# Batch 0 of an attention and expert kernel: summed values brought to their rows by products on TensorE in place of a trip through memory

## The chip, the cores and the metric

The kernel runs on one core of a Trainium2 chip. The metric is device time in microseconds of one execution; the number that counts is the median of several.

## What is computed

The reference first does attention with keys and values that are pooled over eight neighbouring positions, then a two-level mixture of experts on the result. Cut to what matters here:

```python
def _attn_ref(q, k, v):                       # 8 batches, 8 heads, 576 positions, 64 wide
    k_p = k.reshape(B, H, Sp, pool, D).mean(axis=3)      # Sp = 72
    v_p = v.reshape(B, H, Sp, pool, D).mean(axis=3)
    scores = scale * np.matmul(q, k_p.transpose(0, 1, 3, 2))
    ...softmax over the 72 pooled keys...
    return np.matmul(attn, v_p)

def _moe_ref(x, w_group, w_expert, w1, w2):   # x: 4608 tokens, 512 wide
    g_idx = np.argmax(x @ w_group, axis=1)
    ...
        e_idx = np.argmax(xg @ w_expert[g], axis=1)
        ...
            h = np.maximum(xg[mask_e] @ w1[g, e], 0.0)
            out[tok_idx] = combined[:, None] * (h @ w2[g, e])
```

## The kernel before

The eight batches are worked one after the other, and their stages overlap: while batch b runs its expert (class Moe), batch b+1 runs its attention (class Att). For each batch one expert is picked as the main one, and all of the batch's tokens go through it; the few tokens that belong elsewhere are handled at the end by class Left. The expert's two layers are computed at more than single fp32r precision: each weight and each activation is split into a rounded high part and a low part (tiles `wh`, `wl`, and the two halves of `xa` and `xb`), and three products, high by high, low by high and high by low, are summed.

The order of work on every engine is written out by hand, in the strings START, FIRST, SECOND, STEADY and LAST. Each word is a step: `a.sc:0` is method `sc` of batch 0's attention on query chunk 0, `m.` is the expert of the same batch, `n.` the next batch. Each engine works through its own instructions strictly in that order.

The change touches START, which has no expert of an earlier batch to run beside batch 0's attention. The steps of batch 0 there, with the lines of the kernel before, are:

- `vr` (L276, L277, L289, VectorE): sums the values in groups of eight. For batch 0 the sums land in `vf` (a part of a tile named ht), 128 flat rows to a chunk, five chunks; the last chunk begins at row 448.
- `guess_x`, `guess_e` (L508, L516 on TensorE, L511 on ScalarE, L519 to L502 on VectorE): guess the main expert from `vf`. The result `me` is read by SyncE, and only then are the expert's weights loaded (`m.load`, L573, tile sw).
- `home_v` (L224 to L229): brings the sums from `vf` into `v6` (named v in the trace), where each quarter of the 128 partitions holds the rows of two heads, in five groups of 32. The kernel before writes `vf` to memory (vscr) by three SyncE transfers and reads it back by four that ScalarE issues. ScalarE's four wait for the write, so whatever stands behind them on ScalarE waits too.
- `qt` (L315, L311 on TensorE, L317 on ScalarE): turns the queries. `sc` (L336): scores. `mx`, `sb` (L348, L357 on VectorE, L362 on ScalarE): maximum, difference and exponential of a chunk; `sb` is `sd` (the difference) followed by `ex` (the exponential).
- `su_` (L368 to L370, VectorE), `nm` (L375, GpSimd), `pt` (L382, VectorE): sum, norming, transposition of a chunk into pT.
- `vm` (L294, GpSimd): two small products on `v6` that `av` reads.
- `warm:4` (L947): four products of ones with ones, whose result nobody reads.
- `av:0` (L396, TensorE; L401, ScalarE; `avd`, L412, VectorE): the attention's result for the first 256 tokens, tile xa, high and low part.
- `cast` (L579, ScalarE) and `lo` (L585, GpSimd): split a quarter of a weight into its high and low part.
- `m.up` (L602): first layer of the expert; the step of feature block f needs weight quarter f // 2.

GpSimd's order around the change is: `nm` of chunks 0 and 1, `vm`, `lo` of weight quarters 0 and 1, `nm` of chunk 2, `lo` of quarter 2, `nm` of chunk 3, `lo` of quarter 3, `nm` of chunk 4, then the sums of batch 1's values (L276, L277, L289) and batch 1's `vm`, which batch 1's `guess_x` on TensorE reads.

Of the kernel before, what the change touches and what calls it, by code (L numbers as in the profile page):

```python
# [8 lines left out]
F32 = mybir.dt.float32  # L9
# [8 lines left out]
B, H, S, D = 8, 8, 576, 64  # L18
SP = 72
# [15 lines left out]
LATE = 1  # L35
START = """
t.load_wr a.load_k:p a.load_q:0 a.load_vf a.load_q:1 a.load_q:4
t.warm:10 t.turn_wr a.kr:0 a.kr:1 t.split_wr a.kt a.vr:0:f a.vr:1:f a.qt:0 a.qt:1 a.sc:0 a.mx:0 a.sc:1:m t.warm:2 a.guess_x a.sb:0 a.mx:1 a.home_v a.guess_e a.sb:1 a.qt:2 a.su_:0 a.nm:0:p
m.load:1:0 m.load:1:1 m.load:1:2 m.load:1:3 a.qt:3 a.su_:1 a.nm:1:p a.vm a.sc:2:m a.qt:4 t.warm:4 n.load_v n.load_k a.pt:0 a.pt:1 m.cast:1:0 m.lo:1:0:p:4 m.cast:1:1 m.lo:1:1:p:4
a.av:0 a.mx:2 a.sb:2 a.avd:0  # L40
"""
FIRST = """
m.up:0:0:1 a.su_:2 a.nm:2:p m.upd:0:0 a.sc:3 m.cast:1:2 m.load:2:0 m.up:1:0 a.mx:3 a.sb:3 m.lo:1:2:p:4 m.upd:1:0 a.pt:2 m.up:2:0 a.su_:3 a.nm:3:p m.cast:1:3 m.lo:1:3:p:4
m.load:2:1 m.load:2:2 m.upd:2:0 a.sc:4 m.up:3:0 a.mx:4 m.up:4:0 a.sb:4 m.upd:3:0 n.load_qb:0 n.load_qb:1 a.pt:3 a.su_:4 m.upd:4:0 a.nm:4:p m.load:2:3 n.load_qb:2 n.load_qb:3
m.up:5:0 a.pt:4 n.vr:0 m.upd:5:0 m.up:6:0 m.upd:6:0 m.up:7:0 a.av:1 n.vr:1 n.vm a.rt:0 m.upd:7:0 a.avd:1 n.kr:0
m.up:0:1:1 m.upd:0:1 n.kr:1 a.rt:1 n.guess_x m.cast:2:0 m.up:1:1 n.guess_e m.upd:1:1 a.route_g m.cast:2:1 m.up:2:1 m.upd:2:1 a.route_e:p a.gates m.lo:2:0:p:2 m.up:3:1 m.upd:3:1 m.lo:2:1:p:2 m.cast:2:2 m.up:4:1 n.qb:0 m.upd:4:1
# [33 lines left out]
def attn_moe(ctx: ExitStack, tc: tile.TileContext, q, k, v, wg, we, w1, w2, out):  # L80
    nc = tc.nc
# [3 lines left out]
    keep = ctx.enter_context(tc.tile_pool(name="keep", bufs=1))  # L85
    dram = ctx.enter_context(tc.tile_pool(name="dram", bufs=1, space=bass.MemoryType.DRAM))


    ident = keep.tile([128, 128], F32, name="ident")
    make_identity(nc, ident)  # L90
    ones = keep.tile([128, 128], F32, name="ones")
    nc.vector.memset(ones, 1.0)
    rowi = keep.tile([128, 2], F32, name="rowi")
# [48 lines left out]
    gate = keep.tile([128, B, NC], F32, name="gate")  # L142
    loh = keep.tile([128, B, NC, NE], F32R, name="loh")
    xscr = dram.tile([B, 128, 2, 4, S], F32, name="xscr")
    vscr = dram.tile([H * SP + 16, D], F32, name="vscr")

    w1v = w1.rearrange("g e (k p) f -> (g e) p k f", p=128)
    w2v = w2.rearrange("g e (k p) f -> (g e) p k f", p=128)
# [12 lines left out]
    ps_t = ctx.enter_context(tc.tile_pool(name="ps_t", bufs=3, space=PSUM))  # L161


    flat = lambda x: x.rearrange("p h d -> p (h d)")
# [15 lines left out]
    class Att:  # L180
# [40 lines left out]

        def home_v(s):

            nc.sync.dma_start(out=vscr[0:512].rearrange("(t p) d -> p t d", p=128), in_=s.vf[:, 0:4])  # L224
            nc.sync.dma_start(out=vscr[512:576], in_=s.vf[64:128, 4])
            nc.sync.dma_start(out=vscr[576:592], in_=s.vf[0:16, 0])
            for a in range(4):
                o = 2 * SP * a
                nc.scalar.dma_start(out=s.vtile()[32 * a:32 * a + 32, 0:5], in_=vscr[o:o + 160].rearrange("(j i) d -> i j d", i=32))  # L229

        def load_v(s, two=0):

# [768 lines left out]
```

## Time and profile before

| | us |
|---|---|
| median of 3 runs (514.2 to 516.41) | 515.48 |
| the profiled execution | 514.15 |
| its span, first to last instruction | 512.4 |
| TensorE busy in the span | 501.1 |
| GpSimd busy | 281.6 |
| VectorE busy | 345.6 |
| ScalarE busy | 206.3 |

Engines are named PE (TensorE), PEld (its weight loads), DVE (VectorE), ACT (ScalarE), POOL (GpSimd) and SP (SyncE) in the profile; a q behind the name is the engine's queue, which issues transfers. TensorE is busy almost throughout, so a change can save time where TensorE stands idle or repeats itself slowly, which is at the two ends of the span. [...]

### The profile page before, as it was taken

Reading aid. Unit: us, or ns where it says so; the run is one execution under the profiler, and the core shown is the slowest. Engines: PE = TensorE matmul, PEld = TensorE weight load, DVE = VectorE, ACT = ScalarE, POOL = GpSimd, SP = SyncE. Lnnn points to the kernel's source line nnn. Section 1 sums busy time; section 2 is a strip of 40 time slices with the busy share of each in tenths; the row PEclk is TensorE's granted clock in tenths of the full one; section 3 lists DMA queues with packets and bytes.
Section 4 is the critical chain, followed back from the end, with each engine's and each line's share of the span. In section 5 each row is a group of like instructions: output and inputs, shape, how many; then the busy total and the mean of one; then the engine's idle time right before and its main releaser. Section 6 shows DMA issues by size and latency. Waiting matters only on the chain.

```text
span 512.4 us, 14902 instructions
## 1 busy us (share of the span) xinstructions
PE 501.1 (98%) x6085; PEld 440.1 (86%) x6085; DVE 345.6 (67%) x928; ACT 206.3 (40%) x385; POOL 281.6 (55%) x246
## 2 busy tenths in 40 slices
PE   8899999999999999999999999999999999998996
PEld 6688987998889978899789988899789988898976
DVE  6876877899385869486784768476784764199702
ACT  2354432545216542455216551455325551344212
POOL 2386666576518595476828585476947471830400
PEclk9799999999999999999999999999999999999999
DMA  8699299685428966954197615985055100923751
GB/s 279 191 260 205 24 280 236 124 192 137 77 92 242 265 106 176 318 150 80 29 308 213 151 26 138 368 311 89 1 191 192 43 3 22 304 96 114 271 172 58
DMA packets 118110, 83.70 MB, mean 163 GB/s; under 512 B 71034, under 2 KB 93818, under 8 KB 117784
## 3 DMA queue, kind: packets, MB, share of 16 engines
q1 hardware_dynamic: 113408, 75.67, 54.7%
q10 hardware_dynamic: 4600, 7.02, 4.0%
q8 instruction: 49, 0.80, 0.7%
q14 instruction: 21, 0.17, 0.1%
q0 software_dynamic: 32, 0.04, 0.0%
HBM read 77.28 MB, written 28.53 MB: 206 GB/s over the span
## 4 chain that ended last, share of the span: by engine, by line
PE 76%; DVE 10%; DMA 5%; ACT 2%; POOL 2%; issue 2%; SPq 1%; ACTq 0%; DVEq 0%; POOLq 0%
PE mm L602 30%; PE mm L631 27%; PE mm L642 4%; PE sc L396 4%; PE sc L336 4%; DMA vv<-in_v_dram 2%; DMA sw<-in_moe_w_dram 2%; PE tp L429 1%; PE mm L663 1%; POOL w L585 1%; DVE s L368 1%; DVE ht L615 1%; DVE pT L382 1%; PE tp L425 1%; DVE p L357 1%
## 5 line engine op out<-in xcount | busy, mean ns | idle before, releaser
L631 PE MATMUL mm<-w,ht 128*128 128x512 f32 x744 | 172.6, 385 | 0.0
L585 POOL TENSOR_TENSOR w<-sw,w 128x1024 fp32r<-128x1024 f32 (+2 forms) x86 | 145.2, 1711 | 33.7 <-ACT w L579 29.2
L631 PEld LDWEIGHTS mm<-w,ht 128*128 128x128 f32 x744 | 136.8, 189 | 25.2 <-issue 6.4
L602 PE MATMUL mm<-xb,w 128*128 128x288 f32 (+1 forms) x768 | 109.6, 294 | 1.7 <-DVE ht L610 1.7
L602 PEld LDWEIGHTS mm<-xb,w 128*128 128x128 f32 x768 | 100.7, 189 | 6.1 <-ACT w L579 2.2
L602 PE MATMUL mm<-xa,w 128*128 128x288 f32 (+1 forms) x768 | 100.2, 283 | 0.5 <-ACT xa L401 0.5
L602 PEld LDWEIGHTS mm<-xa,w 128*128 128x128 f32 x768 | 95.5, 190 | 2.2 <-ACT xa L401 0.9
L604 ACT ACTIVATE ht<-mm 128x288 fp32r<-128x288 f32 (+2 forms) x128 | 51.9, 410 | 87.1 <-PE mm L602 85.4
L375 POOL TENSOR_TENSOR p<-p,su 128x864 f32<-128x864 f32 (+2 forms) x30 | 40.3, 1343 | 78.6 <-DVE su L370 67.7
L579 ACT CAST w<-sw 128x1024 fp32r<-128x1024 f32 x64 | 66.7, 1042 | 31.5 <-DMA sw<-in_moe_w_dram 29.0
L615 DVE SCALAR_TENSOR_TENSOR ht<-mm,ht 128x64 fp32r<-128x64 f32 (+4 forms) x192 | 37.7, 252 | 25.8 <-ACT ht L604 25.5
L636 ACT ACTIVATE y<-mm,gm 128x512 f32<-128x512 f32 x31 | 21.2, 684 | 66.4 <-PE mm L631 66.4
L362 ACT ACTIVATE p<-p 128x864 f32<-128x864 f32 (+2 forms) x30 | 23.4, 780 | 37.5 <-DVE p L357 29.6
L368 DVE TENSOR_REDUCE s<-p 128x12 f32<-128x864 f32 (+2 forms) x30 | 25.8, 861 | 15.1 <-ACT p L362 15.1
L382 DVE STREAM_TRANSPOSE pT<-p 128x960 f32<-128x960 f32 (+2 forms) x30 | 29.2, 972 | 8.0 <-POOL p L375 7.2
L610 DVE SCALAR_TENSOR_TENSOR ht<-mm,ht 128x288 fp32r<-128x288 f32 (+1 forms) x64 | 26.9, 422 | 10.4 <-ACT ht L604 10.4
L642 PE MATMUL mm<-w,ht 128*128 128x512 f32 x128 | 29.5, 381 | 0.0
L336 PEld LDWEIGHTS sc<-kT,qT 64*32 64x32 f32 x2176 | 23.7, 105 | 6.3 <-issue 3.5
L336 PE MATMUL sc<-kT,qT 64*32 64x72 f32 x2176 | 28.5, 229 | 0.5 <-DVE qT L322 0.2
L675 DVE TENSOR_TENSOR y<-mm,y 64x512 f32<-64x512 f32 x8 | 5.5, 682 | 33.6 <-ACT y L647 20.2
L396 PE MATMUL sc<-pT,v 32*64 32x288 f32 (+2 forms) x384 | 26.9, 409 | 0.2 <-DVE p L357 0.2
L396 PE MATMUL tp<-pT,v 32*64 32x288 f32 (+2 forms) x384 | 26.9, 409 | 0.0
(227 smaller groups left out, 568.8 us busy)
## 6 DMA issues: line engine op xcount, KB each, us to landing
sw<-in_moe_w_dram SPq DMA_DIRECT2D x72, 512.0 KB
vv<-in_v_dram SPq DMA_DIRECT2D x27, 320.0 KB
q<-in_q_dram SPq DMA_DIRECT2D x112, 72.0 KB
kv<-in_k_dram SPq DMA_DIRECT2D x14, 512.0 KB
out_dram<-y ACTq DMA_DIRECT2D x23, 256.0 KB
xscr<-xa SPq DMA_DIRECT2D x5, 1152.0 KB
xscr<-xb SPq DMA_DIRECT2D x5, 1152.0 KB
xscr<-xb SPq DMA_DIRECT2D x3, 1280.0 KB
```

The costliest lines, as they stand in the source:

```text
L336: nc.tensor.matmul(ps[x][32 * g:32 * g + 32, SP * t:SP * t + SP], lhsT=s.qT[c][64 * x:64 * x + 64, g, 32 * t:32 * t + 32], rhs=s.kT[64 * x ...
L368: red(out=two[:, :, :, 0], in_=p.rearrange("p t (x s) -> p t x s", x=2), axis=AX.X, op=ALU.add)
L375: (nc.vector if eng == "v" else nc.gpsimd).tensor_tensor(out=p, in0=p, in1=bc(s.su[c][:, 0:w], SP), op=ALU.mult)
L382: nc.vector.transpose(out=s.pT[:, :, o:o + n].rearrange("p j (t i) -> p t j i", i=32), in_=probs[:, z:z + n // 32].rearrange("p t (j i) -> ...
L396: nc.tensor.matmul(banks[a][64 * x:64 * x + 64, 0:n], lhsT=s.v6[32 * a:32 * a + 32, 5 if x and i == 0 else j, :], rhs=s.pT[32 * a:32 * a + ...
L579: nc.scalar.copy(out=s.w[m, j][0], in_=raw)
L585: (nc.vector if eng == "v" else nc.gpsimd).tensor_tensor(out=wl[:, i:i + n], in0=s.raw[m, j][:, i:i + n], in1=wh[:, i:i + n].bitcast(F32), ...
L602: nc.tensor.matmul(ps[:, 0:n], lhsT=l[:, kc, fs], rhs=apart(s.a.xt[hf][:, r, kc]), start=(kc == 0 and i == 0), stop=(kc == 3 and i == 2))
L604: nc.scalar.activation(out=halves(ht[:, sl]), in_=joined(ps[:, 0:n]), func=AF.Relu)
L615: stt(out=ht[:, at:at + hi - lo], in0=ps[:, a, lo:hi], scalar=0.0, in1=ht[:, t + lo:t + hi].bitcast(F32), op0=ALU.max, op1=ALU.subtract)
L631: nc.tensor.matmul(ps, lhsT=s.ht[f][:, 640 * l + o:640 * l + o + 128], rhs=apart(s.w[2, f // 2][r][:, f % 2, :]), start=(i == 0), stop=(i ...
L642: nc.tensor.matmul(ps, lhsT=s.ht[f][:, 512:640], rhs=apart(s.w[2, f // 2][r][:, f % 2, :]), start=(i == 0), stop=(i == 15))
```

## The change

`home_v` no longer goes through memory. The identity matrix gets 16 columns of zeros on either side (two more memsets on GpSimd), and a window of 32 of its columns, shifted by z, as the stationary operand picks rows z to z + 31 of a chunk of `vf` and puts them on the 32 partitions wanted. Twenty products cover four quarters and five groups, and one group that lies across two chunks takes a second: 21 products, each with 64 columns moving. ScalarE copies the 320 columns of the result to `v6`. With it ScalarE's order changes: the exponential of chunk 1 stands between the two copies of turned queries, and weight quarter 1 is cast after `av:0`'s four results are copied out, and no longer ahead of them. The first `m.up` takes its three products in the order high by high, high weight by low activation, low weight by high activation, where it took the low weight second.

```diff
 START = """
-t.warm:10 ... t.warm:2 a.guess_x a.sb:0 a.mx:1 a.home_v a.guess_e a.sb:1 a.qt:2 a.su_:0 a.nm:0:p
-... a.pt:0 a.pt:1 m.cast:1:0 m.lo:1:0:p:4 m.cast:1:1 m.lo:1:1:p:4
-a.av:0 a.mx:2 a.sb:2 a.avd:0
+t.warm:10 ... t.warm:2 a.guess_x a.sb:0 a.mx:1 a.home_v a.guess_e a.sd:1 a.qt:2 a.ex:1 a.su_:0 a.nm:0:p
+... a.pt:0 a.pt:1 m.cast:1:0 m.lo:1:0:p:4
+a.av:0 a.mx:2 a.sd:2 a.avd:0 m.cast:1:1 m.lo:1:1:p:4 a.ex:2
 FIRST = """
-m.up:0:0:1 a.su_:2 a.nm:2:p m.upd:0:0 ...
+m.up:0:0 a.su_:2 a.nm:2:p m.upd:0:0 ...
-    ident = keep.tile([128, 128], F32, name="ident")
+    identp = keep.tile([128, 160], F32, name="ident")
+    ident = identp[:, 16:144]
     make_identity(nc, ident)
+    nc.gpsimd.memset(identp[:, 0:16], 0.0)
+    nc.gpsimd.memset(identp[:, 144:160], 0.0)
         def home_v(s):
-            nc.sync.dma_start(out=vscr[0:512].rearrange("(t p) d -> p t d", p=128), in_=s.vf[:, 0:4])
-            nc.sync.dma_start(out=vscr[512:576], in_=s.vf[64:128, 4])
-            nc.sync.dma_start(out=vscr[576:592], in_=s.vf[0:16, 0])
-            for a in range(4):
-                o = 2 * SP * a
-                nc.scalar.dma_start(out=s.vtile()[32 * a:32 * a + 32, 0:5], in_=vscr[o:o + 160].rearrange("(j i) d -> i j d", i=32))
+            ps = ps_t.tile([128, 512], F32, name="tp")
+            for j in (3, 0, 1, 2, 4):
+                todo = []
+                for a in range(4):
+                    o = 2 * SP * a + 32 * j
+                    c, z = (4, o - 448) if o >= 448 else (o // 128, o % 128)
+                    todo.append((a, c, z, True, z <= 96 or c == 4))
+                    if z > 96 and c < 4:
+                        todo.append((a, c + 1, z - 128, False, True))
+                for a, c, z, first, last in todo:
+                    nc.tensor.matmul(ps[32 * a:32 * a + 32, D * j:D * j + D], lhsT=identp[:, 16 + z:48 + z], rhs=s.vf[:, c, :], start=first, stop=last)
+            nc.scalar.copy(out=flat(s.vtile()[:, 0:5]), in_=ps[:, 0:5 * D])
```

On TensorE, between the second warming and the scores of chunk 2, the order of before is this (tp and mm are PSUM tiles, hm marks which head a row belongs to, gx is the guess's first result):

```order
L947 MATMUL mm<-ones 128x256 x2
L508 MATMUL tp<-hm,ht 64x4 x10
L516 MATMUL tp<-wr,gx 128x20 x4
L315 MATMUL tp<-ident,q 64x128 x16
L336 MATMUL mm<-kT,qT 32x72 x32
```

And this is the order of the changed kernel at the same place:

```order
L955 MATMUL mm<-ones 128x256 x2
L516 MATMUL tp<-hm,ht 64x4 x10
L236 MATMUL tp<-ht,ident 32x64 x21
L524 MATMUL tp<-wr,gx 128x20 x4
L323 MATMUL tp<-ident,q 64x128 x16
L344 MATMUL mm<-kT,qT 32x72 x32
```

The 21 new products stand between the two halves of the guess, and everything behind them moves back by their time.

On ScalarE, from the copy of gx to the exponential of chunk 2, the order of before is this (p holds the probabilities, v_344 is v6, qT the turned queries, xa the attention's result):

```order
L511 COPY gx<-tp 128x4
L362 ACTIVATE p<-p 128x4x144
L229 DMA v_344<-vscr 32x5x64 x4
L362 ACTIVATE p<-p 128x4x144
L317 COPY qT<-tp 128x4x128 x2
L317 COPY qT<-tp 128x4x64
L579 CAST w<-sw 128x1024 x2
L401 ACTIVATE xa<-sc 128x256 x2
L401 ACTIVATE xa<-tp 128x256 x2
L362 ACTIVATE p<-p 128x4x144
```

And this is the changed kernel's, with v_364 for v6:

```order
L519 COPY gx<-tp 128x4
L370 ACTIVATE p<-p 128x4x144
L237 COPY v_364<-tp 128x320
L325 COPY qT<-tp 128x4x128
L370 ACTIVATE p<-p 128x4x144
L325 COPY qT<-tp 128x4x128
L325 COPY qT<-tp 128x4x64
L587 CAST w<-sw 128x1024
L409 ACTIVATE xa<-sc 128x256 x2
L409 ACTIVATE xa<-tp 128x256 x2
L587 CAST w<-sw 128x1024
L370 ACTIVATE p<-p 128x4x144
```

The four transfers are gone, one copy is there in their place, and the second cast has moved from ahead of the four copies of xa to behind them. VectorE's order has not changed, and GpSimd's only by the memsets at the start.

## Rows read from the trace of the kernel before

**Rows 1.** The page, part 1: busy time, share, instructions; the span above it.

```profile
span 512.4 us, 14902 instructions
PE 501.1 (98%) x6085; PEld 440.1 (86%) x6085; DVE 345.6 (67%) x928; ACT 206.3 (40%) x385; POOL 281.6 (55%) x246
```

**Rows 2.** Waits of TensorE: waiting line, releaser, total, times, longest.

```profile
PE mm L602 <- DVE ht L610: 1.7, 1, 1.7
PE mm L336 <- ACT qT L317: 1.4, 1, 1.4
...
PE mm L602 <- ACT xa L401: 0.5, 1, 0.5
```

**Rows 3.** Timeline of TensorE, 14 to 30 us: start, time, line, shapes, passes, [idle before].

```profile
14.37 0.75 PE L508 MATMUL tp<-hm,ht 128*64 128x4 f32 x20
15.47 1.04 PE L516 MATMUL tp<-wr,gx 128*128 128x20 f32 x8 [0.35 <-ACT gx L511]
16.61 2.64 PE L315 MATMUL tp<-ident,q 128*64 128x128 f32 x32
20.62 1.27 PE L336 MATMUL mm<-kT,qT 64*32 64x72 f32 x64 [1.36 <-ACT qT L317]
...
22.43 3.03 PE L947 MATMUL mm<-ones 128*128 128x256 f32 x8
25.39 0.45 PE L396 MATMUL sc<-pT,v 32*64 32x256 f32 x4
...
27.42 2.10 PE L602 MATMUL mm<-xa,w 128*128 128x256 f32 x12 [0.48 <-ACT xa L401]
```

**Rows 4.** Timeline of ScalarE, 15 to 29 us.

```profile
16.57 2.79 ACTq L229 DMA_DIRECT2D v<-vscr  x4
19.41 0.68 ACT L362 ACTIVATE p<-p 128x576 f32<-128x576 f32 x1 [3.01 <-DMA v<-vscr]
...
24.15 1.05 ACT L579 CAST w<-sw 128x1024 fp32r<-128x1024 f32 x1 [0.24 <-DMA sw<-in_moe_w_dram]
26.98 0.66 ACT L401 ACTIVATE xa<-sc 128x256 fp32r<-128x256 f32 x2 [1.79 <-PE tp L396]
...
28.05 0.71 ACT L362 ACTIVATE p<-p 128x576 f32<-128x576 f32 x1
```

**Rows 5.** Timeline of VectorE, 16 to 24 us.

```profile
16.55 0.18 DVE L519 TENSOR_REDUCE m<-tp 128x5 f32<-128x20 f32 x1
...
17.81 0.81 DVE L357 TENSOR_TENSOR p<-mm,mx 128x288 f32<-128x288 f32 x2
...
22.65 0.84 DVE L382 STREAM_TRANSPOSE pT<-p 128x640 f32<-128x640 f32 x1 [0.61 <-POOL p L375]
```

**Rows 6.** Timeline of GpSimd, 19 to 47 us.

```profile
19.91 1.15 POOL L375 TENSOR_TENSOR p<-p,su 128x576 f32<-128x576 f32 x1 [14.97 <-DVE su L370]
21.46 1.15 POOL L375 TENSOR_TENSOR p<-p,su 128x576 f32<-128x576 f32 x1 [0.41 <-DVE su L370]
...
23.98 5.54 POOL L585 TENSOR_TENSOR w<-sw,w 128x256 fp32r<-128x256 f32 x8 [0.72 <-ACT w L579]
30.34 1.15 POOL L375 TENSOR_TENSOR p<-p,su 128x576 f32<-128x576 f32 x1 [0.82 <-DVE su L370]
...
34.73 1.15 POOL L375 TENSOR_TENSOR p<-p,su 128x576 f32<-128x576 f32 x1 [0.47 <-DVE su L370]
...
45.84 0.82 POOL L294 TENSOR_TENSOR v<-v,share 128x64 f32<-128x64 f32 x2
```

**Rows 7.** Line L294, 0 to 60 us: who waited for it.

```profile
who waited for it (us, times):
  PEld tp L508: 0.2, 1
```

**Rows 8.** Chain that ended last, 0 to 90 us: start, time, what.

```profile
14.25 2.30 DMA vscr<-ht
...
17.44 1.93 DMA v<-vscr
...
46.35 0.33 PE tp L508 x8
46.68 0.03 issue
46.72 0.52 PE tp L508 x12
```

**Rows 9.** Stretches: time, busy of PE, PEld, DVE, ACT, POOL, PEclk, DMA.

```profile
17.90:24.50 6.60, 5.24 (x87) 4.17 (x84) 5.45 (x14) 3.31 (x6) 3.38 (x5) 0.50 0.76 235
24.60:27.40 2.80, 2.34 (x52) 1.38 (x51) 0.33 (x1) 1.01 (x3) 2.80 (x5) 1.00 1.10 311
```

**Rows 10.** Lines of TensorE, 470 to 512 us: products with 32 stationary columns.

```profile
L880 PE MATMUL tp<-sw,q 128*32 128x256 f32 x32 | 1.9, 382 | 0.0
...
L896 PE MATMUL tp<-kv,q 128*32 128x128 f32 x32 | 1.1, 276 | 0.0
```

More of the change, by code (lines that the diff above doesn't have):

```diff
@@ L37 @@
 t.load_wr a.load_k:p a.load_q:0 a.load_vf a.load_q:1 a.load_q:4
-t.warm:10 t.turn_wr a.kr:0 a.kr:1 t.split_wr a.kt a.vr:0:f a.vr:1:f a.qt:0 a.qt:1 a.sc:0 a.mx:0 a.sc:1:m t.warm:2 a.guess_x a.sb:0 a.mx:1 a.home_v a.guess_e a.sb:1 a.qt:2 a.su_:0 a.nm:0:p
-m.load:1:0 m.load:1:1 m.load:1:2 m.load:1:3 a.qt:3 a.su_:1 a.nm:1:p a.vm a.sc:2:m a.qt:4 t.warm:4 n.load_v n.load_k a.pt:0 a.pt:1 m.cast:1:0 m.lo:1:0:p:4 m.cast:1:1 m.lo:1:1:p:4
-a.av:0 a.mx:2 a.sb:2 a.avd:0
+t.warm:10 t.turn_wr a.kr:0 a.kr:1 t.split_wr a.kt a.vr:0:f a.vr:1:f a.qt:0 a.qt:1 a.sc:0 a.mx:0 a.sc:1:m t.warm:2 a.guess_x a.sb:0 a.mx:1 a.home_v a.guess_e a.sd:1 a.qt:2 a.ex:1 a.su_:0 a.nm:0:p
+m.load:1:0 m.load:1:1 m.load:1:2 m.load:1:3 a.qt:3 a.su_:1 a.nm:1:p a.vm a.sc:2:m a.qt:4 t.warm:4 n.load_v n.load_k a.pt:0 a.pt:1 m.cast:1:0 m.lo:1:0:p:4
+a.av:0 a.mx:2 a.sd:2 a.avd:0 m.cast:1:1 m.lo:1:1:p:4 a.ex:2
 """
 FIRST = """
-m.up:0:0:1 a.su_:2 a.nm:2:p m.upd:0:0 a.sc:3 m.cast:1:2 m.load:2:0 m.up:1:0 a.mx:3 a.sb:3 m.lo:1:2:p:4 m.upd:1:0 a.pt:2 m.up:2:0 a.su_:3 a.nm:3:p m.cast:1:3 m.lo:1:3:p:4
+m.up:0:0 a.su_:2 a.nm:2:p m.upd:0:0 a.sc:3 m.cast:1:2 m.load:2:0 m.up:1:0 a.mx:3 a.sb:3 m.lo:1:2:p:4 m.upd:1:0 a.pt:2 m.up:2:0 a.su_:3 a.nm:3:p m.cast:1:3 m.lo:1:3:p:4
 m.load:2:1 m.load:2:2 m.upd:2:0 a.sc:4 m.up:3:0 a.mx:4 m.up:4:0 a.sb:4 m.upd:3:0 n.load_qb:0 n.load_qb:1 a.pt:3 a.su_:4 m.upd:4:0 a.nm:4:p m.load:2:3 n.load_qb:2 n.load_qb:3
@@ L144, in attn_moe @@
     xscr = dram.tile([B, 128, 2, 4, S], F32, name="xscr")
-    vscr = dram.tile([H * SP + 16, D], F32, name="vscr")
     w1v = w1.rearrange("g e (k p) f -> (g e) p k f", p=128)
```

## The prediction

> **What bounds the kernel now.** I read part 1 of the page first: TensorE is busy 501.1 of 512.4 us [rows 1], so time can only be won where it waits or runs slowly. Its waits name the places [rows 2]: the longest stands in the last batch, outside the change (its row names the low part of ht there); the 1.4 us for the turned queries and the 0.5 us for xa lie in the start. So the most that a better start can give is some 2 us, plus what a low clock costs there.
>
> The timelines show how the start hangs together. Behind the guess TensorE turns queries from 16.61, then idles 1.36 us until 20.62 [rows 3]. What it waits for is a copy on ScalarE, and ScalarE stood still for 3.01 us, until 19.41, because its four transfers from memory had to wait for the write [rows 4]; the chain shows both legs, 2.30 and 1.93 us [rows 8]. That is the stall that the change removes. Yet `av:0` does not start when its inputs are there: chunk 1 is transposed by 22.65 + 0.84 = 23.49 [rows 5], and TensorE comes to `av:0` at 25.39, because the warming products, 3.03 us for 8 passes, stand ahead of it [rows 3]. [...]
>
> A second engine is as tight as TensorE. GpSimd runs from 30.34 to 46.66 with one gap, 0.47 us [rows 6], and its last piece there, batch 1's `vm` (45.84 + 0.82 = 46.66), releases TensorE's guess for batch 1: L508 breaks off at 46.68 and goes on at 46.72 [rows 8], and the line's own view names the weight load of L508 as waiting [rows 7]. So at 46.7 us the two engines arrive together, and TensorE can keep only as much gain as GpSimd also makes. From there TensorE's waits are small until the last batch, and I carry a shift at 46.7 us to the end.
>
> **The change, part by part.** *The 21 products* are 42 passes, since each product shows as two (x32 passes for 16 products of L315). The trace has none with this shape. Nearest are those with 32 stationary columns: L896 takes 1.1 us for 32 passes of 128 columns, L880 1.9 us for 32 of 256 [rows 10]. Half the columns, about half the time: so 64 columns would be about 15 ns a pass, 0.6 us in all, if that goes on; if it stops at 128 columns, 1.1 / 32 = 34 ns, 1.4 us. L508, whose four columns leave only its load of 64 stationary columns, takes 0.75 / 20 = 38 ns [rows 3]; half the columns to load would be 19 ns. I take 19 ns, 0.8 us, with 0.6 and 1.4 as the ends.
>
> *What they delay.* They run while TensorE would have idled 0.35 us for gx [rows 3], so the guess's second half moves back by 0.8 - 0.35 = 0.45 us (0.25 to 1.05). VectorE's order has the guess ahead of chunk 1's difference [rows 5], so that difference, the sums and chunk 0's norming follow at +0.45: 19.91 becomes 20.36. SyncE's weight loads wait for the guess too, +0.45; the second quarter, for which its cast waited until 24.15 [rows 4], is there at 24.6, before it is wanted now.
>
> *What they win.* Chunk 1's exponential no longer waits for memory, so GpSimd norms chunk 1 straight behind chunk 0, without the gap of 0.41 us [rows 6]: start 21.51, end 22.66, transposed by 23.5. Against 23.49 nothing is won there; what is won is that TensorE need no longer be late. From the guess's end to `av:0` it has 16.61 to 25.39 less the wait of 1.36, 7.4 us at mostly the low clock. [...] I take 23.55, 1.85 us earlier than 25.39.
>
> *ScalarE's copy* of 320 columns lies where the exponential of chunk 0 has ended and TensorE is still turning queries: a copy of 256 columns takes some 0.3 us (four xa copies between 26.98 and 28.05 [rows 4]). I cost it at nothing; without that cover it would be 0.4 us. The two memsets come in the first 2 us, ahead of loads that VectorE waits for anyway: nothing, or their own 0.1 us.
>
> *The moved cast* costs. Before, GpSimd's eight low-part pieces ran from 23.98, 5.54 us, and then waited 0.82 us until 30.34 [rows 6]. Now quarter 1 is cast behind the copies of xa: `av:0` to its first copy 26.98 - 25.39 = 1.59, four copies 28.05 - 26.98 = 1.07, the cast 1.05, half of the eight pieces 2.77 [rows 3, 4, 6]: chunk 2's norming can start 6.5 us after `av:0`, where it started 4.95 after. At 23.55 that is 30.05, only 0.3 earlier than 30.34. The 0.47 us gap before 34.73 closes as well, since its release by VectorE follows TensorE, which is more than 1 us earlier by then. In one formula: GpSimd's gain at its last piece is (25.39 - start of `av:0`) - (6.5 - 4.95) + 0.47, so the gain in `av:0`'s start less 1.08 us. With 1.85: 0.75 us.
>
> *The order of the first* `m.up` decides whether it waits last for low weights or for low activations. The step takes 2.10 us [rows 3], so less than that is at stake; GpSimd's chain, which TensorE meets later, covers it, and I give it nothing.
>
> *The sum.* TensorE reaches its first `m.up` 1.85 us earlier, then gives 1.1 us of it back, at GpSimd's low parts or at the latest at `vm`, and keeps 0.75. The profiled execution's 514.15 becomes 513.4; it ran 1.33 us under the median of 515.48, so the median becomes 514.7. With the ends of the products' cost, 0.6 and 1.4 us, the gain is 0.95 and 0.15: 514.5 to 515.3.
>
> **The rivals.** [...]
>
> *The four quarters' products run side by side.* Were they to overlap as fully as L396 does, whose 24 products of 256 columns (three by four by two in the code) take 1.6 us, from 25.39 to 26.98 [rows 3, 4], the 42 passes would cost 0.3 us and delay nothing: `av:0` at 23.1, a gain of 2.3 - 1.08 = 1.2, median 514.3. Against it: L896 and L880 already use four quarters and reach 34 and 59 ns. [...]
>
> *GpSimd does not hold TensorE back.* Were the meeting at 46.7 us chance, and the low parts ready early enough, the whole 1.85 us would stay: median 513.6. Rows 7 speak against it.
>
> **How the numbers follow.** The forecast has 0.52, the low clock 0.2, the full overlap 0.1, the full gain 0.08; 0.1 is left for shifts elsewhere (transfers that start 0.45 us later, three runs that spread over 2.2 us). The likeliest is 514.7. The low clock ends at 516.0, the full gain at 513.6; with half a microsecond for the median's own spread the range is 513.1 to 516.6. A change of 0.5% (2.6 us) is about what a measurement of this kernel can tell from none; no case reaches it, so only the rest does: faster 0.05, same 0.91, slower 0.04.
>
> **What would show it.** The products: 42 passes in about 0.8 us between the two halves of the guess. ScalarE without a 3 us wait; `av:0` near 23.5, released by chunk 1's transposition; clock at 1.00 for most of 18 to 24 us. GpSimd's norming of chunk 2 near 30.0 and batch 1's `vm` ending near 45.9; TensorE waiting for `vm` at its guess for batch 1. I am wrong if `vm` ends later than 46.66, if `av:0` still follows the warming at 25 us, or if TensorE gets past 46 us without waiting for `vm`.

## The result and the profile after

The changed kernel takes 517.44 us (median of 9 runs, 515.96 to 518.66), the kernel before 514.2 us beside it (9 runs, 512.41 to 517.39). The ratio is 1.0056, 95% interval 1.0034 to 1.0078: slower by 0.56%, some 2.9 us of 514.2 (the two medians lie 3.2 us apart), where 0.8 us less was forecast. The time lies above the range. The profiled execution took 516.02 us, 1.4 under its median, so it shows too little of the loss; a second one is among the runs.

Part 1 of the page after, span and busy times, answers to [rows 1]:

```profile
span 514.3 us, 14972 instructions
PE 501.7 (98%) x6127; PEld 439.9 (86%) x6127; DVE 345.9 (67%) x928; ACT 207.1 (40%) x386; POOL 281.6 (55%) x248
```

TensorE has 42 matmuls and 42 weight loads more. Its busy time grew by 0.6 us, the span by 1.9: the rest is waiting. Of TensorE's waits (line, releaser, total, times, longest) these are new, or longer than in the kernel before, where the first was 0.2 us in all [rows 2]:

```profile
PE sc L344 <- DVE qT L330: 1.6, 2, 1.0
PE sc L404 <- DVE pT L390: 1.3, 1, 1.3
...
PE tp L236 <- issue: 0.6, 1, 0.6
...
PE mm L610 <- issue: 0.3, 1, 0.3
```

"issue" as a releaser means that the engine waited for nothing that the profile shows. The timeline of TensorE (answers to [rows 3]) has the first of these stops in the middle of the new products:

```profile
15.12 0.75 PE L516 MATMUL tp<-hm,ht 128*64 128x4 f32 x20
15.80 0.42 PE L236 MATMUL tp<-ht,ident 128*32 128x64 f32 x9
16.84 0.69 PE L236 MATMUL tp<-ht,ident 128*32 128x64 f32 x33 [0.62 <-issue]
17.46 1.07 PE L524 MATMUL tp<-wr,gx 128*128 128x20 f32 x8
18.46 1.97 PE L323 MATMUL tp<-ident,q 128*64 128x128 f32 x32
20.36 1.09 PE L344 MATMUL mm<-kT,qT 64*32 64x72 f32 x64
...
25.11 0.45 PE L404 MATMUL sc<-pT,v 32*64 32x256 f32 x4 [1.34 <-DVE pT L390]
```

ScalarE's and GpSimd's timelines (answer to [rows 4, 6]):

```profile
17.57 0.43 ACT L237 COPY v<-tp 128x320 f32<-128x320 f32 x1 [0.90 <-PE tp L236]
...
24.62 1.04 ACT L587 CAST w<-sw 128x1024 fp32r<-128x1024 f32 x1 [2.32 <-DMA sw<-in_moe_w_dram]
```

```profile
31.68 1.16 POOL L383 TENSOR_TENSOR p<-p,su 128x576 f32<-128x576 f32 x1
...
46.65 0.81 POOL L302 TENSOR_TENSOR v<-v,share 128x64 f32<-128x64 f32 x2
```

The chain of waits leads from the guess through SyncE's queue to batch 1's first scores:

```profile
20.78 0.41 SPq L581
...
25.50 14.01 DMA vv<-in_v_dram
...
39.52 1.18 SPq L272
...
55.53 3.06 DMA q<-in_q_dram
...
59.53 0.87 PE sc L344 x48
```

The weight load that stands at 20.78 stood at 18.77 in SyncE's timeline of before. Behind it, in the same queue, come batch 1's values and keys, the second layer's weights and batch 1's queries; before, the last of these were issued by 46.84 + 5.12 = 51.96 us, now by 51.32 + 4.71 = 56.03. SyncE's timelines, before and then after:

```profile
18.77 2.13 SPq L573 DMA_DIRECT2D sw<-in_moe_w_dram  x4
...
46.84 5.12 SPq L264 DMA_DIRECT2D q<-in_q_dram  x8
```

```profile
20.78 2.18 SPq L581 DMA_DIRECT2D sw<-in_moe_w_dram  x4
...
51.32 4.71 SPq L272 DMA_DIRECT2D q<-in_q_dram  x8
```

One part of every difference in the start has nothing to do with the change. TensorE's first work, 20 warming passes that are the same in every kernel, took 6.02 us in the profile of before and 7.13 in that of after:

```profile
1.15 6.02 PE L947 MATMUL mm<-ones 128*128 128x256 f32 x20 [1.15 <-DVE ones L92]
```

```profile
1.15 7.13 PE L955 MATMUL mm<-ones 128*128 128x256 f32 x20 [1.15 <-DVE ones L95]
```

In the 17 profiles of the experiments they took 6.25 to 7.55 us, in kernels with and without the change. So the guess begins 0.75 us later in the profile of after (15.12 against 14.37), before the first new product runs. In the profiles without padding near 8 us it begins between 14.25 and 15.54, and 14.37 is the second earliest.

### The profile page after: what moved, and what is told of

Same layout as the page of the kernel before. It is cut to its first block, busy times and chain, and to the rows that moved or that the text cites. A ratio compares the mean times of both kernels' runs of the same rounds, so it can differ in the third digit from the quotient of the medians.

```text
span 514.3 us, 14972 instructions
## 1 busy us (share of the span) xinstructions
PE 501.7 (98%) x6127; PEld 439.9 (86%) x6127; DVE 345.9 (67%) x928; ACT 207.1 (40%) x386; POOL 281.6 (55%) x248
## 4 chain that ended last, share of the span: by engine, by line
PE 86%; SPq 4%; DVE 4%; DMA 3%; ACT 1%; issue 1%; ACTq 0%; DVEq 0%
PE mm L639 32%; PE mm L610 30%; PE mm L650 5%; PE sc L344 5%; PE sc L404 4%; DMA vv<-in_v_dram 3%; SPq L272 3%; PE mm L955 2%; PE tp L437 1%; PE mm L671 1%; PE tp L433 1%; SPq L581 1%; DMA q<-in_q_dram 1%; PE tp L307 1%; PE tp L470 1%
```

## The experiments

I put the shift of each kernel against the profile of before into one table: start of the same TensorE instruction, counted from the last one, less its start in before, in us; a negative number is a gain. The columns are six places of before's time, TensorE's last instruction (last), the difference of the two spans (end, which holds what comes behind TensorE's last instruction too), and the step from 110 to 126. The first columns hold the chance of the first warming, up to 1.2 us; the step from one late column to the next does not.

```
TensorE instructions added  28     47     58    110    126    171   last    end  110 to 126
 +84 after               -0.29   0.80   1.87   1.67   1.63   2.05   2.03   1.95   -0.04
 +84 e12 (after again)   -0.39   1.56   2.49   2.29   2.90   3.84   4.85   4.94    0.61
 +84 e1                  -0.97   0.07   0.07   0.06   0.82   1.29   1.95   1.88    0.76
 +84 e2                   0.60   1.05   1.05   1.02   1.71   2.12   2.94   3.08    0.69
 +84 e5                  -2.05  -1.60  -1.61  -1.57  -1.10  -0.45   0.20   0.36    0.47
 +84 e15                 -0.41   1.34   1.33   1.31   1.41   1.87   2.65   2.64    0.09
 +84 e4                  -0.44  -0.16   0.48   0.28   0.34   0.78   0.90   1.00    0.06
 +84 e6                   3.81   3.80   3.80   3.81   4.64   5.18   5.21   5.97    0.83
 +84 e13                 -0.57  -0.27   0.33   0.12   0.99   1.44   1.37   2.10    0.87
   0 e3                  -1.16  -0.12  -0.12  -0.13  -0.14  -0.07  -0.06   0.70   -0.01
   0 e10                 -1.38  -0.78   0.02  -0.18  -0.24  -0.53  -0.52  -0.69   -0.06
   0 e11                  0.20   1.60   1.60   1.60   1.60   2.47   2.45   2.46    0.00
   0 e14                 -1.07  -0.25  -0.25  -0.26  -0.25   0.58   0.48   0.31    0.01
+256 e7                   4.26   5.30   6.64   6.45   6.38   7.43   7.70   7.62   -0.06
+256 e8                   4.60   5.67   5.67   5.69   5.69   5.66   6.00   5.97    0.00
+256 e16                 -0.05   4.53   4.53   4.54   4.55   4.78   5.17   5.20    0.01
+256 e17                  0.73   4.99   4.99   5.03   5.02   4.88   4.99   5.66    0.00
+256 e18                  2.66   4.79   4.79   4.82   4.82   5.15   5.09   5.08    0.00
```

### The change with parts undone

**e1**: the guess's second half ahead of the new products.

```diff
-... a.home_v a.guess_e a.sd:1 ...
+... a.guess_e a.home_v a.sd:1 ...
```

> The changed kernel with the 21 products moved behind the guess's second half on TensorE; all else as changed. Late guess (theory 1: the products delay the guess, so SyncE's weight loads and every transfer queued behind them): the weight loads start near 18.8 to 19.5 us instead of 20.78, batch 1's queries land 2 us or more earlier, the 1.0 us wait of the scores near 59 us goes, and the time falls by 2 to 3.5 us from the changed kernel's 517.4, to before's or under it. Moved cast (theory 2: the cast behind xa's copies holds GpSimd up): at most 0.5 us of change, the time stays near 517. Early clock (theory 3: the warming at the start ran slower by chance): no change beyond the spread of runs.

Measured: 1.0034 (1.0016 to 1.0052), median 515.98, 1.5 us under the changed kernel where 2 to 3.5 were expected. SyncE's loads begin at 19.06, and the wait at 58 us is gone. At 110 us TensorE is level with before, and loses 0.76 us by 126. Its mean granted clock from 17.90 to 22.00 was 0.58, where the changed kernel had 1.00, so the two differ by more than the place of the guess.

**e2**: the cast and low parts of quarter 1 put back ahead of the copies of xa.

```diff
-... a.pt:1 m.cast:1:0 m.lo:1:0:p:4
-a.av:0 a.mx:2 a.sd:2 a.avd:0 m.cast:1:1 m.lo:1:1:p:4 a.ex:2
+... a.pt:1 m.cast:1:0 m.lo:1:0:p:4 m.cast:1:1 m.lo:1:1:p:4
+a.av:0 a.mx:2 a.sd:2 a.avd:0 a.ex:2
```

> The changed kernel with the cast of weight quarter 1 ahead of xa's copies again, as before the change. Late guess: the weights land late, so ScalarE waits for quarter 1 with xa's copies behind it, and the time is the same or up to 1 us worse than the changed kernel's. Moved cast: 1 us or more faster than the changed kernel. Early clock: no change.

Measured: 1.0082 (1.0052 to 1.0112). The two casts (25.29 and 26.65) wait 3.55 and 0.31 us for weights, and the first copy of xa comes at 27.60, behind them; the move keeps the changed kernel's own late loads away from these copies.

**e5**: both, on one kernel.

> The changed kernel with the products behind the guess and the cast of quarter 1 ahead of xa's copies, so the products and the copy are all that is left of the change. Late guess theory (products ahead of the guess delay every transfer): with the guess early both are right, TensorE is 0.5 to 1 us earlier than before at 47 and 58 us, and the time is 0 to 1 us under before's. Code position theory (the 84 extra instructions on TensorE shift the places where it loads its code, into a stretch dense with products and on top of weight transfers): TensorE still stops for its code near 120 us and a cast near 157 us waits longer for weights, so the time stays 0.5 to 2 us over before's whatever the start gains.

Measured: 1.0047 (1.0031 to 1.0064). Its profile, the fastest of its runs (514.43 against a median of 515.91), has TensorE 1.57 us ahead at 110 us, and all of it is lost behind: 0.47 to 126 us, 0.65 to 171, 0.65 to TensorE's last instruction and 0.16 behind that.

**e3**: the kernel before with only the moved cast and the changed order of the first `m.up`.

> The kernel before, round trip kept, with only the changed orders: cast of quarter 1 behind xa's copies, and the first up step's three products in the changed order. Late guess: within 0.5 us of before or up to 1 us slower, since the guess stays early. Moved cast: 1 to 3 us slower than before, most of what the change cost. Early clock: no change.

Measured: 1.0012 (0.9999 to 1.0024), a gain of 1.16 us at 28 us that is 0.12 at 47.

### Products that nobody reads

**e4**: the kernel before, with 21 products of the new shape between the halves of the guess; the trip through memory stays.

```diff
+        def dead_v(s):
+            ps = ps_t.tile([128, 512], F32, name="tp")
+            for i in range(21):
+                a, j = i % 4, i // 4
+                nc.tensor.matmul(ps[32 * a:32 * a + 32, D * j:D * j + D], lhsT=ident[:, 32 * a:32 * a + 32], rhs=s.vf[:, i % 5, :], start=True, stop=True)
-... a.home_v a.guess_e a.sb:1 ...
+... a.home_v a.dead_v a.guess_e a.sb:1 ...
```

> The kernel before, round trip and orders kept, with 21 products of home_v's shape, whose result nobody reads, between the two halves of the guess. Late guess: 1 to 3 us slower than before, with weight loads starting 1 us or more later than 18.77 and batch 1's queries late. Moved cast: within 0.7 us of before, since only TensorE gets some 0.8 us more work. Early clock: no change.

Measured: 1.0049 (1.003 to 1.0068). It has a loss like the changed kernel's, without its new path; its profile, 1.2 us under its median, shows only 1.0 us of it.

**e13**: the same products where TensorE waits 1.36 us for turned queries [rows 3], behind the guess.

```diff
-... a.vm a.sc:2:m ...
+... a.vm a.dead_v a.sc:2:m ...
```

> The kernel before with 21 products of the new shape whose result nobody reads, put where TensorE waits 1.36 us for the turned queries. Guess and weight loads are not delayed, and about 0.85 us of products hides in that wait, so whatever is lost comes from the 84 instructions that stand ahead of all later ones and move the code loads of TensorE. If the moved code loads cost by themselves: stops of 0.2 to 0.6 us near 112 and 120 us, released by nothing that the profile shows, and later weights near 169 us, in all 0.5 to 1.3 us, ratio 1.001 to 1.0025. If only the late guess and the late transfers cost: ratio 0.999 to 1.0005 and no shift after 100 us.

Measured: 1.0037 (1.0017 to 1.0057), some 1.9 us, more than the 1.0025 that I had as the upper end. The products do not delay the guess, they lie in a wait, and the loss is there. TensorE's timeline:

```profile
19.51 0.86 PE L235 MATMUL tp<-ht,ident 128*32 128x64 f32 x42
21.03 0.89 PE L342 MATMUL mm<-kT,qT 64*32 64x72 f32 x64 [0.66 <-ACT qT L323]
...
118.89 1.05 PE L608 MATMUL mm<-xa,w 128*128 128x256 f32 x7
120.84 2.16 PE L608 MATMUL mm<-xa,w 128*128 128x256 f32 x17 [0.91 <-issue]
```

A hundred microseconds behind the added products, in code that the edit does not touch, TensorE stops for 0.91 us and waits for nothing that the profile shows. In the kernel before the same 24 passes run in one piece:

```profile
118.58 2.94 PE L602 MATMUL mm<-xa,w 128*128 128x256 f32 x24
```

Where TensorE stops is told by counting: matmuls, weight loads and sequencer instructions of TensorE up to the first one behind the stop.

```
stops "<-issue" of over 0.1 us: time (length) instruction number, and that modulo 256
after  16.84 (0.62)  449: 193    121.81 (0.29) 3520: 192
e12    16.74 (0.92)  449: 193    115.72 (0.54) 3265: 193    123.08 (0.18) 3520: 192
e1    120.89 (0.74) 3521: 193
e2     16.48 (0.14)  449: 193    114.16 (0.24) 3265: 193    121.89 (0.55) 3520: 192
e4     16.45 (0.11)  449: 193
e5     20.31 (0.43)  704: 192    111.60 (0.29) 3264: 192    118.97 (0.15) 3521: 193
e6     16.48 (2.10)  448: 192    116.94 (0.26) 3265: 193    124.60 (0.63) 3520: 192
e7     15.57 (2.31)  448: 192
e8     15.76 (2.24)  448: 192
e13   120.84 (0.91) 3521: 193
e15   121.58 (0.42) 3520: 192
e16    25.80 (0.67)  961: 193
e17    26.58 (1.38)  961: 193     36.44 (2.27) 1216: 192
e18    28.40 (1.47)  961: 193
before, e3, e10, e11, e14: none
```

Each of the 24 stops falls at the same place of a block of 256. Part 3 of the changed kernel's page has a queue that fits (name, kind, packets, MB, share):

```profile
q8 instruction: 49, 0.80, 0.7%
```

0.80 MB in 49 packets are 16 KB each, which would be 64 bytes for each of 256 instructions. So I read these stops as loads of TensorE's code. In the changed kernel the queue's first packet runs from 14.06 to 15.43 us, and the first stop ends 1.4 us behind it, at 16.84; in e13 one runs from 118.24 to 119.29, ahead of 120.84. The queue's records bear this out in all 19 profiles. Give the k-th packet to the block that begins at instruction 256 k + 193: no block's first instruction starts less than 1.19 us after its packet has ended, and all 24 stops end 1.2 to 1.7 us after theirs. The five kernels below with 256 instructions more have 50 packets, the fourteen others 49.

### Padding to a whole block

If the place in the block is what costs, 172 instructions more (43 products of 16 columns, two passes each, 86 matmuls and 86 loads) make 256 and put all later code back into its old place. **e7** is the changed kernel and **e8** e1 with this padding, near 8 us; **e6** is the kernel before with 21 such products there.

```diff
+        def pad(s, z):
+            ps = ps_m.tile([128, 512], F32, name="mm")
+            for i in range(z):
+                a = i % 4
+                nc.tensor.matmul(ps[32 * a:32 * a + 32, 0:16], lhsT=ones[:, 0:32], rhs=ones[:, 0:16], start=True, stop=True)
-t.warm:10 t.turn_wr a.kr:0 ...
+t.warm:10 t.turn_wr t.pad:43 a.kr:0 ...
```

> The kernel before with 21 tiny products of ones in TensorE's idle time near 8 us, their result unread: 84 more instructions on TensorE, as in the change, and nothing else. Late guess theory: within 0.4 us of before. Code position theory: shifts as in the change behind 110 us, 0.5 to 1 us in the profile (a stop near 120 us, a longer wait near 171 us), and 0.5 to 1.5 us in the median.

> The changed kernel with 43 tiny products of ones near 8 us: 172 more instructions, 256 more than before in all, so that TensorE's code loads fall where they fell before. Late guess theory alone: no faster than the changed kernel. Code position theory: the stop near 121 us and the longer wait near 172 us go, the time is 0.5 to 1.5 us under the changed kernel's; the late queries near 58 us stay.

> The changed kernel with the products behind the guess and 43 tiny products near 8 us. Late guess theory alone: as the run with the guess first, some 1.9 us over before. Code position theory: within 0.7 us of before or under it, since both costs are gone.

Measured: 1.0149 (1.012 to 1.0179), 1.0111 (1.0091 to 1.0131), 1.0136 (1.0115 to 1.0157). As a remedy this failed: TensorE now reaches instruction 448 while its code is still under way (in e6 it stops at 14.38 us, and the packet ends at 15.19). The row of e6, and two of its stretches (busy times, then the granted clock):

```profile
16.48 0.33 PE L336 MATMUL mm<-kT,qT 64*32 64x72 f32 x9 [2.10 <-issue]
```

```profile
8.00:16.00 8.00, 5.83 (x205) 4.81 (x204) 5.79 (x12) 3.62 (x7) 0.00 (x0) 1.00 0.85 256
17.30:27.40 10.10, 9.75 (x132) 8.35 (x131) 5.15 (x18) 2.63 (x6) 2.27 (x3) 0.50 0.31 87
```

**e16** (e1), **e17** (e5) and **e18** (e13) have the same padding where TensorE waits before `av:0`.

```diff
-... a.qt:4 t.warm:4 n.load_v ...
+... a.qt:4 t.warm:4 t.pad:43 n.load_v ...
```

> The changed kernel with the guess first and 43 further products of 16 columns, which nobody reads, put where TensorE waits about 1.3 us for chunk 1 ahead of the first results of attention. They take about 0.9 us, which that wait hides. With the 84 instructions of the change they make 256, so that every later instruction lies again where it lay in its block of 256. If the place in the block is what costs: no stop and no step of TensorE's shift between 58 us and 175 us, where the same kernel without them had 1.2 us, and a ratio of 0.999 to 1.001 against 1.0034. If the number of instructions costs, or something else in the start: 1.0034 or more. The price of a stop of up to 1 us in the start, where small products read code quickly, would show near 24 us.

> The same with the cast and the low parts of weight quarter 1 back ahead of the results of attention, where the profile without the padding had TensorE 1.6 us ahead of the kernel before at 110 us and lost 2 us in steps behind it. If these steps are code loads and go with the padding: 0.5 to 1.5 us faster than before, ratio 0.997 to 0.999. If not: 1.003 to 1.005 as without the padding.

> The kernel before with the 21 products in TensorE's wait and the 43 small ones behind the warming, 256 instructions together. If the place in the block is what costs, the steps near 112 to 126 us and at 169 us are gone and the ratio is 0.999 to 1.001, against 1.0037 with the 21 products alone. If the number of added instructions costs, 1.0037 or more.

Measured: 1.0072 (1.0048 to 1.0096), 1.0068 (1.0046 to 1.0091), 1.01 (1.0063 to 1.0137). The ratios miss what I expected. At 47 us the three are 4.5 to 5.0 us late, where the same kernels without padding were between 1.6 us early and 0.1 us late. They stop at instruction 961 and again at 1216, and in each the granted clock is 0.50 for a stretch behind one of the two stops (from 38 to 40 us in e16 and e17, behind the second; from 30 to 32 us in e18, behind the first). In e16 and e18 the profile puts the second stop, 2.54 and 1.09 us, down to GpSimd's low parts, but there too it ends 1.51 us after its packet. e17's timeline of TensorE shows the second stop:

```profile
31.44 2.72 PE L610 MATMUL mm<-xa,w 128*128 128x256 f32 x22
36.44 0.38 PE L610 MATMUL mm<-xa,w 128*128 128x256 f32 x2 [2.27 <-issue]
```

Behind the start, though, all five kernels with 256 do what the theory of the place says: the step from 110 to 126 us is -0.06 to 0.01, as in the four without added instructions (-0.06 to 0.01), while the nine with 84 lose -0.04 to 0.87, 0.48 on average (4.34 / 9). So it is the place that counts there, and not the number of added instructions. Nor is it that the added products take a result tile out of a pool of three, and so shift the tiles of all later ones: e6 takes another tile (mm) than e13 (tp) and has the same step, and e18 takes both and has none. e18's timeline has the stretch where e13 stopped in one piece, as it is in the kernel before:

```profile
123.40 2.94 PE L608 MATMUL mm<-xa,w 128*128 128x256 f32 x24
```

### The stall removed without a product

**e10**: the kernel before, its four reads issued by GpSimd, which has nothing to do there, and the exponential of chunk 1 between the copies of turned queries.

```diff
-... a.guess_e a.sb:1 a.qt:2 a.su_:0 ...
+... a.guess_e a.sd:1 a.qt:2 a.ex:1 a.su_:0 ...
-                nc.scalar.dma_start(out=s.vtile()[32 * a:32 * a + 32, 0:5], ...
+                nc.gpsimd.dma_start(out=s.vtile()[32 * a:32 * a + 32, 0:5], ...
```

> The kernel before, with the trip through memory kept, but its four reads are issued by GpSimd, which has nothing to do there, and ScalarE goes on to the copies of the turned queries (exponential of chunk 1 between the two copies). No product is added on TensorE and the guess is not delayed, so SyncE's loads start where they do in the kernel before. If the loss of the changed kernel comes from its 84 instructions on TensorE (the guess later by their time, the code loads moved into dense stretches), this kernel has none of it: no stop of TensorE for its code near 112 and 120 us, SyncE's first weight load near 18.8 us, the 1.36 us wait for the turned queries gone, and the time equal to before or up to 2 us less (ratio 0.996 to 1.000). If the loss comes from ScalarE's and GpSimd's changed times in the start (the rival), it stays here: ratio 1.003 or more.

Measured: 1.0001 (0.9987 to 1.0014). The start is as the prediction wanted it, `av:0` at 23.87 and no wait for turned queries, and the runs show no gain from it. Timelines of TensorE, and of VectorE and TensorE near 57 us:

```profile
19.12 0.89 PE L336 MATMUL mm<-kT,qT 64*32 64x72 f32 x64
...
23.87 0.45 PE L396 MATMUL sc<-pT,v 32*64 32x256 f32 x4 [1.55 <-DVE pT L382]
```

```profile
56.82 0.71 DVE L322 STREAM_TRANSPOSE qT<-q 128x512 f32<-128x512 f32 x1 [1.12 <-DMA q<-in_q_dram]
...
57.67 0.88 PE L336 MATMUL sc<-kT,qT 64*32 64x72 f32 x64 [0.74 <-ACT w L579]
```

TensorE is 1.38 us early at 28 us and 0.78 at 47; then batch 1's scores wait until their queries have landed and been transposed, and 0.02 late is what is left. The last row names a cast (L579), which ended just before the scores began. But the transposition ended at 56.82 + 0.71 = 57.53, 0.14 before them, and in the changed kernel too the chain has 0.14 between the two (59.39 to 59.53). In e14, below, the same scores start while that cast still runs, so they do not need it (ScalarE, then TensorE):

```profile
57.10 1.07 ACT L579 CAST w<-sw 128x1024 fp32r<-128x1024 f32 x1
```

```profile
57.40 0.88 PE L336 MATMUL sc<-kT,qT 64*32 64x72 f32 x64
```

Two things weaken e10's profile as a witness. Its guess begins 0.78 us later than in before, by the first warming, and with it SyncE's loads (19.55 against 18.77) and so the queries. And its span ends 0.69 us ahead of before's all the same, while the two kernels take equal time. What decides is the ratio.

**e11**: the same four reads issued by SyncE, ahead of the weight loads (`nc.sync.dma_start`).

> The same with the four reads issued by SyncE. They wait for the write in SyncE's queue ahead of the expert's weights, so the weight loads start about 0.5 to 1.5 us later than in the kernel before, with TensorE's instructions unchanged. If the late transfers alone are what costs, the time is 0.5 to 1.5 us above the run with GpSimd, and batch 1's first scores wait for turned queries near 58 us as in the changed kernel. If the moved code loads alone cost, it is equal to the run with GpSimd.

Measured: 1.0041 (1.0023 to 1.0059) with not one instruction more on TensorE. The loads begin at 20.09. The second cast waits for its weights, and since it stands ahead of the copies of xa, it holds TensorE up. The rows of ScalarE and TensorE:

```profile
26.24 1.04 ACT L579 CAST w<-sw 128x1024 fp32r<-128x1024 f32 x1 [1.17 <-DMA sw<-in_moe_w_dram]
```

```profile
27.62 2.24 PE L602 MATMUL mm<-xa,w 128*128 128x256 f32 x12 [2.40 <-ACT xa L401]
```

I had looked for the loss at 58 us; it came at 27.6.

**e14** is e10 and **e15** the changed kernel, both with batch 1's last eight query transfers ahead of the last quarter of the second layer's weights.

```diff
-... m.load:2:3 n.load_qb:2 n.load_qb:3
+... n.load_qb:2 n.load_qb:3 m.load:2:3
```

> The kernel before with its four reads issued by GpSimd, and SyncE issuing the last eight query transfers of batch 1 ahead of the last quarter of the second layer's weights, not behind it. Without the second edit TensorE was 1.4 us early at 28 us and 0.8 us early at 47 us, and level again at 58 us. If batch 1's queries, last in SyncE's queue, set the time there, they land 0.5 to 1.5 us earlier and TensorE keeps 0.5 to 0.8 us at 58 us, unless the cast of the last weight quarter now waits: ratio 0.998 to 0.9995. If something else sets it, TensorE is level with the kernel before at 58 us again: ratio 1.000.

> The changed kernel with the same exchange in SyncE's queue: batch 1's last eight query transfers ahead of the last quarter of the second layer's weights. If the late transfers are what costs at 58 us, the wait of 1.01 us for turned queries goes or falls below 0.4 us, and the ratio against before falls from 1.0056 to about 1.003 to 1.0045. If they are not, it stays at 1.0056.

Measured: 1.0 (0.9982 to 1.0017) and 1.0078 (1.0056 to 1.0099). The wait at 58 us went in both, and nothing was won: e14 had 1.07 us at 28 us and kept 0.25 at 47 (one of its waits there is 0.9 us for GpSimd's low parts), and e15 was 1.3 us late by 47. So the queries' wait is one of several, and taking it away alone returned nothing that these runs can tell.

**e12**: the changed kernel again.

> The changed kernel once more, as a second profile. The first profile ran 516.02 us where the median of its runs is 517.44. If the 1.4 us lie in the start (transfers that come later by chance), TensorE's shift against the first profile shows up before 60 us and stays; if they lie in code loads that stop TensorE by chance, it shows as stops released by nothing that the profile shows, at the same instructions as in the first profile (0.3 to 0.8 us each, near 15.8, 112 and 120 us).

Measured: 519.0 us, one execution. Against the first profile it is 0.76 us later at 47 us, 1.27 at 126, 1.79 at 171 and 2.99 at the end: it loses in the start and in the later steps, and in no single one. The stop amid the new products is there again, at the same instruction. Two of its waits of TensorE:

```profile
PE tp L237 <- issue: 0.9, 1, 0.9
PE sc L345 <- issue: 0.5, 1, 0.5
```

## Why the prediction was wrong

In short: the prediction had most parts of the start right, one by one. But it took a gain at 47 us for a gain at the end, it had no term for what instructions added to TensorE cost beyond their own time, and it took the guess's delay for smaller than it was and for covered. The second of these made most of the loss. The prediction's own first sign of being wrong came true: `vm` ended at 47.46, later than 46.66.

| step of the prediction | forecast | measured |
|---|---|---|
| 42 passes | 0.8 us | 0.86 in one piece (e13) |
| guess's second half later | 0.45 us | 17.46 - 15.47 = 1.99, of which 15.12 - 14.37 = 0.75 came before the products |
| copy of 320 columns | hidden, 0.4 uncovered | 0.43, under the guess's second half |
| wait for the turned queries | gone | gone |
| `av:0` | 23.55 | 25.11 (23.87 in e10) |
| clock from 17.90 to 24.50 | 1.00 for most | 1.00 |
| norming of chunk 2 after `av:0` | 6.5 us | 31.68 - 25.11 = 6.57 |
| `vm`: gain of `av:0` less 1.08 | 45.9 | 0.28 - 1.08 = -0.80; 46.65 + 0.81 = 47.46, 0.80 later |
| first weight load | +0.45, covered | 20.78 - 18.77 = 2.01, 0.75 of it from before the products; cast waits 2.32 |
| 84 instructions more on TensorE, beyond their time | no term | 0.37% (e13) |

The rows fit together: `av:0` came 25.11 - 23.55 = 1.56 us later than forecast, and 0.75 us of late start and 1.24 - 0.45 = 0.79 us more delay of the guess make 1.54.

**What held.** The price of a pass, the covered copy, the stall that goes, and the formula for GpSimd. That the formula gives `vm` to a hundredth is luck: chunk 2's norming came 6.57 us after `av:0` and not 6.5, and from there to the end of `vm` GpSimd took 15.78 us where it had taken 16.32, 0.54 less and not 0.47. The two errors cancel. The 23.55 of the sum rests also on my estimate that TensorE is past its warming by 23.5, and no run of the change shows it: `av:0` came at 25.11. What that profile shows is that the eight warming passes began at 21.77 and took 1.99 us, where before they took 3.03 [rows 3], and that TensorE then waited 1.34 us for chunk 1. The low clock, which has 0.2 of the chances and 516.0 as its end, is not what this profile shows: the stretch from 17.90 to 24.50 in the changed kernel, last but two the clock, against 0.50 before [rows 9]:

```profile
17.90:24.50 6.60, 5.87 (x114) 4.80 (x113) 5.06 (x17) 2.21 (x5) 2.51 (x3) 1.00 0.40 130
```

Nor do the products run side by side: 0.86 / 42 = 20 ns a pass, not the 7 ns of that rival.

**The step that would have failed without any loss** is the sum's last: "From there TensorE's waits are small until the last batch, and I carry a shift at 46.7 us to the end." e10 has the gain without any of the costs, 0.78 us at 47, which would be 0.15%, and a ratio of 1.0001, whose interval just leaves that out; e3 and e14, with 1.0012 and 1.0, agree. So these runs show no gain that lasts. Small waits show where TensorE has slack in that one order, not how much earlier it could run. VectorE's transposition of batch 1's queries starts at 56.40 in before without a wait:

```profile
56.40 0.70 DVE L322 STREAM_TRANSPOSE qT<-q 128x512 f32<-128x512 f32 x1
```

But the transfers that it needs had been issued until 51.96, and nothing in the change made them earlier. And by 47 us e3, e10 and e14 have lost part of what they had at 28, before the queries matter. Which of these takes the gain in a usual run is not shown.

**The term that was not in the sum** made most of the loss. I counted instructions of TensorE as time only. 84 more of them, hidden in a wait, cost 0.37% (0.17 to 0.57) in e13, and leaving them where they are but sparing the guess leaves 0.34% (0.16 to 0.52) in e1. The place of later code in its blocks is shown as the cause of stops in the start and of 0.48 us on average from 110 to 126 us. That the rest of e13's 1.9 us comes from it is not shown. e13's profile loses 0.45 us from 126 to 171 and 0.73 behind TensorE's last instruction, and such steps occur without added instructions too (0.83 from 126 to 171 in e14, 0.76 behind the last instruction in e3). From 171 us to TensorE's last instruction the four kernels without added instructions lose nothing (-0.10 to 0.01), and the nine with 84 lose -0.07 to 1.01, 0.44 on average, with no stop of this kind there; the cause of that stays open. The padded kernels, whose start is some 5 us late, can't settle it in their ratios.

**The term that was mis-sized** is the guess's delay: 0.45 us forecast, 1.24 measured, of which 0.62 is the code stop that fell between the two halves. And it was called covered ("before it is wanted now"). That held for quarter 1's cast, but quarter 0's waited 2.32 us, and the second layer's weights and batch 1's queries stand behind the loads in SyncE's queue: TensorE's wait of 1.01 us for these queries is there in the changed kernel and gone in e1. Its price is the difference of two ratios, 0.56 - 0.34 = 0.22% from the changed kernel and e1, 0.49 - 0.37 = 0.12% from e4 and e13: the same sign twice, but each less than the intervals can tell from nothing.

No version beat the kernel before: e10 and e14, with 1.0001 and 1.0, equal it.

## What to carry to other kernels

Before a gain in the start is carried to the end, look for the next place where work meets something that did not get earlier, a transfer queue above all; a cheap version that makes only the gain (here e10) tells it before the costly one is written. Work put ahead of an instruction that releases a queue delayed here all that stood in the queue, even where the work filled a wait (the first weight load from 18.77 to 20.78 us, the end of the last queries' issue from 51.96 to 56.03, 0.75 us of each from before the products); put behind it, it took one wait away and won 0.12 to 0.22%, not clear of noise. On an engine that runs thousands of short instructions, added ones can cost more than their time (here 84, hidden in a wait, came with 0.37%, e13): look in the waits for stops that nothing releases, and count where in the code they fall. And before two profiles are laid side by side, take off what they differ by ahead of the change.

## What the runs showed of the hardware

- TensorE's stops without a releaser fall at instruction numbers of 192 or 193 modulo 256, all 24 of them, 0.11 to 2.31 us long; the queue "instruction" moves 16 KB a packet, 49 or 50 of them, which fits one for 256 instructions, and each stop ends 1.2 to 1.7 us after the packet of its block. The queue's first packet starts between 13.0 and 14.4 us in every kernel.
- The five kernels with 43 added products of 16 columns, 0.91 or 0.92 us of work, had stops of 0.67 to 2.31 us in the start.
- The granted clock was 0.50 for 10.1 us after the 2.10 us stop in e6, and in the changed kernel 1.00 through the same stretch (17.3 to 27.4 us).
- The first 20 warming passes of TensorE, the same in every kernel, took 6.02 to 7.55 us in the 19 profiles.
